# Float32 weight forms and the sums' places in a tile of their own

## The chip, the core and the metric

The kernel runs on one core of one Trainium2 chip. The metric is the device time of one execution in microseconds. A core has a matrix engine (PE, TensorE), three engines for elementwise work (DVE is VectorE, ACT is ScalarE, POOL is GpSimd), and a queue for transfers (SP, SyncE); ACT issues transfers as well. Each engine works through its own list of instructions in order and waits on semaphores where a value of another engine is needed. PE reads its operands from on-chip memory (128 partitions) and writes sums to PSUM. In the profile PEld is the loading of a weight into PE, an instruction of its own.

## What is computed

Causal attention over a window of 128 positions with a slope for each head, then a feed-forward layer in which two projections are multiplied:

```
scores = scale * q @ k.T                       # 8 batches, 8 heads, 576 positions, 64 wide
scores = where(0 <= rel < 128, scores - slopes * abs(rel), -1e9)
attn   = exp(scores - max);  attn = attn / (sum(attn) + 1e-9)
x      = attn @ v                              # -> 4608 tokens x 512
out    = ((x @ w_a) * (x @ w_b)) @ w_out       # 512 -> 1536 -> 512
```

The weights arrive as 64-bit floating point numbers and the result is float32.

## The kernel before, in words

**Batches.** The eight batches are worked one after the other, and the attention of batch b + 1 runs beside the feed-forward layer of batch b. The attention of batch 0 stands alone at the start (its lines are around 520 to 680), and beside it the weights are prepared. The feed-forward layer of batch 0 is `first_up` (twelve strips f of 128 hidden columns, 48 matmuls each: two halves of the tokens, two weights, and 12 partial products) and `first_down`. Later batches use `up_plain` or `up_fast` for each strip and `down` behind it. A product of two fp16 numbers split in a high and a low part takes three matmuls (high x high, high x low, low x high); `terms` issues the six of one block of weights against one block of x, for both k halves.

**The tile of weights.** `wup` holds, for each of the 12 strips, seven blocks of weights; a block is 128 columns for two k halves, each as a high and a low fp16 part (L83). Blocks 0 to 3 are the weights themselves: `w_a` in 0 and 1, `w_b` in 3 and 2. Blocks 4 to 6 are sums and differences of these, which only `up_fast` reads. That function makes a strip from seven products in place of eight, and is used for the first six strips of batch 2, ten strips of batch 3 and all strips from batch 4 on. A strip of blocks 4 to 6 is therefore free in the first two batches, and the kernel uses it for other things.

**From 64 bits to fp16.** A load n brings 1024 raw 64-bit numbers a partition into `raws[n % 3]`, which lies in the tile of the down weights, `wdn`. Loads 0 to 11 are strips of up weights, 12 to 17 pairs of strips of down weights. `convert(n)` makes float32 bit patterns from them in three DVE instructions (L130, L132, L133), written to `forms[n % 6]`. `forms[n]` is blocks 4 and 5 of strips 2n **and** 2n + 1 of `wup`: two runs of 512 float32 numbers a partition, with the blocks 6 of the first strip and 0 to 3 of the second between them.

```
wup = const.tile([P, NF, 7, 2, 2, P], F16, name="wup")
forms = [wup[:, 2 * n:2 * n + 2, 4:6, :, :, :].rearrange("p m a c k f -> p m (a c k f)").bitcast(F32) for n in range(NF // 2)]
```

For up weights ACT squares the forms (L139), PE sums the squares (L155), DVE and POOL make a power of two from the largest (L160 and `power_scale`), and `split_up` writes the fp16 parts into blocks 0 to 3 (ACT L147 the high part, DVE L148 the low one). For down weights one scale serves all: `down_weights` adds up all squares, sends the sum through a matmul with ones into the tile `wtot` (L100 and L101), works out `ratio` (L225), and then splits strip by strip into `wdn` (L229 on ACT, L230 on DVE), which overwrites the raws.

**Sums.** `sums_of_weights` makes blocks 4 to 6 in batches 1 to 3. For each strip and each k half POOL adds the high and low part of blocks 0 to 3 in float32 (L246) and forms block 3 again and the three new ones (L247 to L250); ACT writes the four high parts into blocks 3 to 6 with one copy of 4 x 128 numbers a partition (L255), and DVE the four low parts with one subtraction (L256). POOL's float32 results need a place for a while: for strips below 8 that is one of four `spare` places, in blocks 4 and 5 of strips 8 to 11, in turn, later a work tile `ws32`.

**Order.** SP's list is in the order of the source for the first batch, and PE's list for all later batches. All other lists are put in order by a scheduler that simulates the time of each instruction and takes the waits between instructions into account. Such a wait is made where two accesses overlap in a tile.

**Attention, as far as it appears below.** For a pair of heads: load q and k; for batches from 2 on, square and sum (L322), scale and split into `qkh` and `qkl` (L339, L340), and lay the parts out anew with transfers (L348 to L351); scores on PE (L376 for batch 1, L380 later); bias and maximum on DVE (L384); exponential on ACT (L385); normalize (`rin`: L394, L398) and split into the fp16 parts of `phl` (L401 on ACT, L402 on DVE); one transfer that transposes `phl` into `pT`; the product with v on PE (L503); and out of PSUM on ACT (L416). In the feed-forward layer L788 and L790 take the up products out of PSUM into `rc` (the hidden values), and L844 and L845 split these into h.

Of the kernel before, what the change touches and what calls it, by code (L numbers as in the profile page):

```python
# [11 lines left out]
F32 = mybir.dt.float32  # L12
F16 = mybir.dt.float16
# [5 lines left out]
ALU = mybir.AluOpType  # L19
# [3 lines left out]
DM, DF = 512, 1536  # L23
P = 128
NPAIR = H // 2
NKC = DM // P
NF = DF // P
NE = DM // P
HT = S // 2
# [17 lines left out]
def attention_then_bilinear_ffn(ctx: ExitStack, tc: tile.TileContext, qT, kT, vP, w_a, w_b, w_out, rel, slopes2, outT):  # L47
    nc = tc.nc
    vec, act, pe, pool, sp = nc.vector, nc.scalar, nc.tensor, nc.gpsimd, nc.sync

    const = ctx.enter_context(tc.tile_pool(name="const", bufs=1))
# [28 lines left out]

    wup = const.tile([P, NF, 7, 2, 2, P], F16, name="wup")  # L83
    wdn = const.tile([P, NF, 2, DM], F16, name="wdn")

    raws = [wdn[:, 4 * n:4 * n + 4, :, :].rearrange("p a c f -> p (a c f)").bitcast(I64).rearrange("p (m n) -> p m n", m=2) for n in range(3)]
    forms = [wup[:, 2 * n:2 * n + 2, 4:6, :, :, :].rearrange("p m a c k f -> p m (a c k f)").bitcast(F32) for n in range(NF // 2)]
    xs = const.tile([P, 8, 2, 2, HT], F16, name="xs")
    sup = const.tile([P, NF, 2], F32, name="sup")
    ratio = const.tile([P, NF], F32, name="ratio")  # L90
# [112 lines left out]
    def down_weights():  # L203

        sums = small.tile([P, NF // 2], F32, tag="wos", name="wos", bufs=1)
        for n in range(NF // 2 + 1):
            conv = convert(NF + n) if n < NF // 2 else iter(())
            next(conv, None)
            yield
            next(conv, None)  # L210
            if n:
                squares(NF + n - 1, accum_out=sums[:, n - 1:n])
                if n + 2 < NF // 2:
                    load_weights(NF + n + 2, (w_out[2 * n + 4], w_out[2 * n + 5]), sp)
            yield
        sab = small.tile([P, NF], F32, tag="sab", name="sab", bufs=1)
        vec.tensor_tensor(out=sab, in0=sup[:, :, 0], in1=sup[:, :, 1], op=ALU.mult)
        vec.tensor_reduce(out=smin, in_=sab, op=ALU.min, axis=AX)
        vec.reciprocal(sab, sab)
        s1 = small.tile([P, 1], F32, tag="wo1", name="wo1", bufs=1)  # L220
        vec.tensor_reduce(out=s1, in_=sums, op=ALU.add, axis=AX)
        tot = ps_at.tile([P, 512], F32, tag="at", name="wtot")
        total(tot[:, 0:1], s1)
        power_scale(so, tot[:, 0:1], 1.01, 15)
        vec.tensor_scalar(out=ratio, in0=sab, scalar1=smin, scalar2=so, op0=ALU.mult, op1=ALU.mult)  # L225
        yield
        for f in range(NF):
            s, x = ratio[:, f:f + 1], forms[f // 2][:, f % 2, :]
            act.activation(wdn[:, f, 0, :], x, AF.Copy, scale=s)  # L229
            vec.scalar_tensor_tensor(out=wdn[:, f, 1, :], in0=x, scalar=s, in1=wdn[:, f, 0, :], op0=ALU.mult, op1=ALU.subtract)  # L230
            yield

    def sums_of_weights():


        spare = cycle([wup[:, f, 4:6, :, :, :].rearrange("p a c k f -> p (a c k f)").bitcast(F32).rearrange("p (s f) -> p s f", s=4) for f in range(8, NF)])

        def place():
            return next(spare) if f < 8 else work.tile([P, 4, P], F32, tag="t", name="ws32", bufs=4)

        late = []
        for f, k in [(f, k) for f in range(NF) for k in range(2)] + [(None, None)] * 1:
            if f is not None:
                a, z = place(), place()
                with tc.issue_after(last_bias[0].ins):
                    pool.tensor_tensor(out=a, in0=wup[:, f, 0:4, 0, k, :], in1=wup[:, f, 0:4, 1, k, :], op=ALU.add)  # L246
                pool.tensor_tensor(out=z[:, 0, :], in0=a[:, 3, :], in1=a[:, 2, :], op=ALU.add)  # L247
                pool.tensor_tensor(out=z[:, 2, :], in0=a[:, 0, :], in1=a[:, 3, :], op=ALU.subtract)
                pool.tensor_tensor(out=z[:, 1, :], in0=z[:, 0, :], in1=a[:, 0, :], op=ALU.subtract)
                pool.tensor_tensor(out=z[:, 3, :], in0=a[:, 1, :], in1=z[:, 1, :], op=ALU.subtract)  # L250
            late.append((f, k, z))
            if len(late) > 1:
                g, m, x = late.pop(0)
                with tc.issue_after(last_main[0].ins):
                    act.copy(wup[:, g, 3:7, 0, m, :], x)  # L255
                vec.tensor_tensor(out=wup[:, g, 3:7, 1, m, :], in0=x, in1=wup[:, g, 3:7, 0, m, :], op=ALU.subtract)  # L256
            yield


# [587 lines left out]
    def terms(ps, a, b, first, last):  # L847

        ks = [(k, wi, xi) for k in range(2) for wi, xi in ((0, 0), (0, 1), (1, 0))]
        for n, (k, wi, xi) in enumerate(ks):  # L850
            pe.matmul(ps[:, 0:HT], wup[:, a[0], a[1], wi, k, :], xs[:, b, xi, k, :], start=(first and n == 0), stop=(last and n == len(ks) - 1), skip_group_check=True)  # L851

    def up_plain(st, f, h):

# [221 lines left out]
```

## Time and profile before

| | |
|---|---|
| median of 3 runs | 999.38 us (998.4 to 1001.05) |
| the profiled execution, its own time | 1000.43 us |
| its span in the trace | 998.6 us |
| mean clock granted to PE | 0.987 |
| instructions | 23811 |
| moved by transfers | 102.82 MB, 103 GB/s on average |

The engines' busy time by stage, in us, from the windows of the trace:

| stage (us of the span) | length | PE | DVE | ACT | POOL | clock |
|---|---|---|---|---|---|---|
| 0 to 120, attention of batch 0, most weights | 120 | 108.08 | 98.04 | 88.09 | 21.05 | 0.94 |
| 120 to 165, first up projection | 45 | 34.80 | 42.88 | 33.91 | 8.07 | 0.89 |
| 165 to 210, first down projection | 45 | 44.33 | 25.48 | 25.95 | 6.96 | 1.00 |
| 210 to 460, batches 1 to 3 in the main, with the sums | 250 | 244.81 | 181.35 | 175.23 | 103.01 | 1.00 |
| 460 to 998.6, the rest | 538.6 | 532.91 | 319.98 | 310.54 | 116.42 | 1.00 |

The span is the time from the first to the last recorded instruction; the execution's own time is a little longer. A row of the timeline or of a group names the engine, the tiles written and read (written<-read), the line in the kernel and the number of instructions. An instruction that had to wait carries in brackets how long and for which instruction. L12 is line 12 of the kernel.

### The profile page before, as it was taken

How to read it: one execution, taken by the hardware profiler on the slowest of the kernel's cores; microseconds unless marked ns; L12 is line 12 of the kernel's file. 1: busy time of each engine (PE TensorE's matmuls, PEld its weight loads, DVE VectorE, ACT ScalarE, POOL GpSimd, SP SyncE). 2: the span in 40 equal slices, each digit the busy share in tenths (PEclk: the TensorE clock that was granted, in tenths of full speed). 3: DMA queues.
4: the chain of work that ended last, by engine and by line, in shares of the span. 5: the costliest groups of instructions: out<-in, count | busy, mean ns of one | idle time of the engine just before them, and what ended most of it. 6: DMA issues, size and time to landing. Idle time of an engine off the chain costs nothing.

```text
span 998.6 us, 23811 instructions
## 1 busy us (share of the span) xinstructions
PE 964.9 (97%) x9339; PEld 749.9 (75%) x9339; DVE 667.7 (67%) x1843; ACT 633.7 (63%) x1705; POOL 255.5 (26%) x309
## 2 busy tenths in 40 slices
PE   7899959999999999999999999999999999999998
PEld 5567747777877777777777777777777777877776
DVE  5979999468878567786778677666677476524530
ACT  5967769567666757766776867677666766413321
POOL 1211212022655312452226123121223022211100
PEclk8999979999999999999999999999999999999999
DMA  8424753474346343473533643374335532210001
GB/s 316 170 110 189 230 154 61 110 187 84 65 97 139 95 90 70 86 178 75 99 75 96 160 91 65 76 192 107 68 72 97 161 67 44 49 37 8 1 13 36
DMA packets 148432, 102.82 MB, mean 103 GB/s; under 512 B 120032, under 2 KB 128352, under 8 KB 147296
## 3 DMA queue, kind: packets, MB, share of 16 engines
q1 hardware_dynamic: 138816, 91.77, 37.8%
q10 hardware_dynamic: 9504, 9.54, 3.0%
q8 instruction: 73, 1.20, 0.5%
q14 instruction: 39, 0.32, 0.1%
HBM read 48.33 MB, written 9.44 MB: 58 GB/s over the span
## 4 chain that ended last, share of the span: by engine, by line
PE 69%; DVE 14%; DMA 7%; ACT 6%; issue 3%; SPq 0%; POOL 0%; ACTq 0%; DVEq 0%
PE ch L851 19%; PE dn_ps L947 16%; PE p L851 14%; PE up_ps L851 11%; PE x_ps L503 4%; PE sc_ps L380 3%; DMA v<-in_vP 3%; DVE phl L402 2%; DMA pT<-phl 2%; PE dn_ps L814 2%; DVE wup L133 1%; DVE wup L148 1%; DVE wup L132 1%; DVE t L384 1%; ACT vsq L278 1%
## 5 line engine op out<-in xcount | busy, mean ns | idle before, releaser
L851 PEld LDWEIGHTS <-wup 128*128 128x128 f16 x4224 | 408.9, 98 | 125.3 <-DVE wup L133 10.5
L947 PE MATMUL dn_ps<-h,wdn 128*128 128x288 f16 x2016 | 254.4, 286 | 0.0
L947 PEld LDWEIGHTS <-wdn 128*128 128x128 f16 x2016 | 194.0, 98 | 51.8
L851 PE MATMUL ch<-xs,wup 128*128 128x288 f16 x1536 | 221.8, 286 | 1.8 <-ACT rc L876 1.3
L851 PE MATMUL up_ps<-xs,wup 128*128 128x288 f16 x1536 | 196.6, 288 | 11.0 <-DVE wup L133 10.2
L851 PE MATMUL p<-xs,wup 128*128 128x288 f16 x1152 | 172.6, 286 | 0.0
L906 POOL TENSOR_TENSOR rc<-rc,row 128x288 f32<-128x288 f32 x64 | 62.5, 976 | 279.7 <-DVE row L904 263.7
L385 ACT ACTIVATE t<-t,mn 128x192 f32<-128x192 f32 (+2 forms) x252 | 107.1, 427 | 25.2 <-DVE mn L384 25.0
L402 DVE SCALAR_TENSOR_TENSOR phl<-t,rin,phl 128x192 f16<-128x192 f32 (+2 forms) x252 | 107.5, 467 | 19.7 <-ACT phl L401 19.5
L844 ACT CAST h<-rc 128x576 f16<-128x576 f32 x96 | 64.2, 669 | 70.3 <-DVE rc L911 36.7
L401 ACT ACTIVATE phl<-t,rin 128x192 f16<-128x192 f32 (+2 forms) x252 | 88.8, 425 | 31.1 <-DMA pT<-phl 17.7
L845 DVE TENSOR_TENSOR h<-rc,h 128x576 f16<-128x576 f32 x90 | 69.0, 767 | 31.1 <-ACT h L844 30.1
L384 DVE CUSTOM_DVE_ANT_0 t<-sc_ps,bias,neg 128x192 f32<-128x192 f32 (+2 forms) x216 | 73.8, 390 | 8.0 <-PE sc_ps L380 7.9
L438 DVE TENSOR_TENSOR xs<-v,xs 128x576 f16<-128x576 f32 x52 | 49.0, 955 | 22.3 <-ACT xs L437 22.1
L952 ACT ACTIVATE row<-dn_ps,oi 128x288 f32<-128x288 f32 x56 | 27.6, 494 | 55.9 <-PE dn_ps L947 55.8
L888 ACT ACTIVATE row<-ch,g 128x288 f32<-128x288 f32 x64 | 31.8, 497 | 48.8 <-PE ch L851 48.8
L883 DVE TENSOR_TENSOR rc<-p,rc 128x288 f32<-128x288 f32 x64 | 29.1, 455 | 44.1 <-PE p L851 34.6
L361 POOL TENSOR_SCALAR bias<-rel_sb,ninv,sl_sb 128x192 f32<-128x192 f32 x24 | 20.3, 844 | 121.6 <-DVE mn L384 121.6
L432 POOL TENSOR_TENSOR xq<-xq,sq 128x576 bf16<-128x576 bf16 x22 | 29.5, 1341 | 83.7 <-ACT sq L431 83.7
L911 DVE SCALAR_TENSOR_TENSOR rc<-rc,g,ch 128x288 f32<-128x288 f32 x64 | 32.7, 511 | 23.6 <-PE ch L851 23.4
L385 ACT ACTIVATION_READ_ACCUMULATOR t<-t,mn 128x1 f32 x252 | 47.6, 189 | 0.0
L437 ACT CAST xs<-v 128x576 f16<-128x576 f32 x52 | 34.1, 668 | 16.6 <-POOL v L456 9.4
(148 smaller groups left out, 1260.3 us busy)
## 6 DMA issues: line engine op xcount, KB each, us to landing
v<-in_vP SPq DMA_DIRECT2D x8, 1280.0 KB, 6.5
out<-row ACTq DMA_DIRECT2D x62, 144.0 KB, 1.8
qk<-in_qT SPq DMA_DIRECT2D x28, 288.0 KB, 4.1
qk<-in_kT SPq DMA_DIRECT2D x28, 288.0 KB, 4.6
wdn<-in_w_a SPq DMA_DIRECT2D x12, 512.0 KB, 5.1
wdn<-in_w_b SPq DMA_DIRECT2D x12, 512.0 KB, 5.9
wdn<-in_w_out SPq DMA_DIRECT2D x12, 512.0 KB, 4.4
qst<-qkh SPq DMA_DIRECT2D x24, 144.0 KB, 2.8
```

The costliest lines, as they stand in the source:

```text
L384: vec.tensor_tensor_reduce(out=t[:, c:c + w], in0=ps[:, c:c + w], in1=o.bias[:, WIN - w:WIN], scale=-0.125 if o.b == 1 else o.neg, scalar= ...
L385: act.activation(t[:, c:c + w], t[:, c:c + w], AF.Exp, bias=o.mn[:, n:n + 1], scale=-1.0, accum_out=o.sm[:, n:n + 1])
L401: act.activation(phl[:, 0, pc:pc + w], e, AF.Copy, scale=s)
L402: vec.scalar_tensor_tensor(out=phl[:, 1, pc:pc + w], in0=e, scalar=s, in1=phl[:, 0, pc:pc + w], op0=ALU.mult, op1=ALU.subtract)
L437: act.copy(xs[:, n, 0, :, :], src)
L438: vec.tensor_tensor(out=xs[:, n, 1, :, :], in0=src, in1=xs[:, n, 0, :, :], op=ALU.subtract)
L503: last = pe.matmul(xp[oc // 512][64 * h:64 * h + 64, o0:o0 + w], vt[0:rows, c:c + 64], probs(pt, rows, blocks, h), start=(n == 0 and first ...
L844: act.copy(h[:, f, :, 0, :], hid)
L845: eng.tensor_tensor(out=h[:, f, :, 1, :], in0=hid, in1=h[:, f, :, 0, :], op=ALU.subtract)
L851: pe.matmul(ps[:, 0:HT], wup[:, a[0], a[1], wi, k, :], xs[:, b, xi, k, :], start=(first and n == 0), stop=(last and n == len(ks) - 1), ski ...
L906: pool.tensor_tensor(out=x0, in0=x0, in1=mid, op=ALU.mult)
L947: pe.matmul(ps[:, 0:HT], wdn[:, f, wi, e * P:(e + 1) * P], h[:, f, t, hi, :], start=(m == 0 and n == 0), stop=(m == NF - 1 and n == 2))
```

## The change

`wup` keeps four blocks a strip. Blocks 4 to 6 become blocks 0 to 2 of a new tile `wsum` with the same twelve strips. Seen as float32, `wsum` is one run of 9216 numbers a partition, here named `flat`. The forms are now nine pieces of 1024 in a row, which fill it exactly, in place of six pairs of strips. Load n goes to `forms[n % 9]`, and `down_weights` reads load 12 + k at `forms[(12 + k) % 9]`. The spare places are the last third of `flat`, strips 8 to 11 with all their blocks, as six pieces of 512 in place of four.

Since block 3 and blocks 4 to 6 of a strip now lie in two tiles, the copy and the subtraction at the end of `sums_of_weights` are each made twice: 128 numbers a partition for block 3, 384 for the others. There are 24 of each pair, so 24 more instructions on ACT and 24 more on DVE. `terms` chooses the tile by the block's number. Nothing that is computed changes.

```diff
--- before.py
+++ after.py
@@ -80,11 +80,13 @@
 
 
 
-    wup = const.tile([P, NF, 7, 2, 2, P], F16, name="wup")
+    wup = const.tile([P, NF, 4, 2, 2, P], F16, name="wup")
+    wsum = const.tile([P, NF, 3, 2, 2, P], F16, name="wsum")
     wdn = const.tile([P, NF, 2, DM], F16, name="wdn")
 
     raws = [wdn[:, 4 * n:4 * n + 4, :, :].rearrange("p a c f -> p (a c f)").bitcast(I64).rearrange("p (m n) -> p m n", m=2) for n in range(3)]
-    forms = [wup[:, 2 * n:2 * n + 2, 4:6, :, :, :].rearrange("p m a c k f -> p m (a c k f)").bitcast(F32) for n in range(NF // 2)]
+    flat = wsum.rearrange("p f a c k q -> p (f a c k q)").bitcast(F32)
+    forms = [flat[:, 2 * DM * n:2 * DM * n + 2 * DM].rearrange("p (m f) -> p m f", m=2) for n in range(9)]
     xs = const.tile([P, 8, 2, 2, HT], F16, name="xs")
     sup = const.tile([P, NF, 2], F32, name="sup")
     ratio = const.tile([P, NF], F32, name="ratio")
@@ -225,7 +227,7 @@
         vec.tensor_scalar(out=ratio, in0=sab, scalar1=smin, scalar2=so, op0=ALU.mult, op1=ALU.mult)
         yield
         for f in range(NF):
-            s, x = ratio[:, f:f + 1], forms[f // 2][:, f % 2, :]
+            s, x = ratio[:, f:f + 1], forms[(NF + f // 2) % len(forms)][:, f % 2, :]
             act.activation(wdn[:, f, 0, :], x, AF.Copy, scale=s)
             vec.scalar_tensor_tensor(out=wdn[:, f, 1, :], in0=x, scalar=s, in1=wdn[:, f, 0, :], op0=ALU.mult, op1=ALU.subtract)
             yield
@@ -233,7 +235,7 @@
     def sums_of_weights():
 
 
-        spare = cycle([wup[:, f, 4:6, :, :, :].rearrange("p a c k f -> p (a c k f)").bitcast(F32).rearrange("p (s f) -> p s f", s=4) for f in range(8, NF)])
+        spare = cycle([flat[:, n:n + 4 * P].rearrange("p (s f) -> p s f", s=4) for n in range(8 * 6 * P, 12 * 6 * P, 4 * P)])
 
         def place():
             return next(spare) if f < 8 else work.tile([P, 4, P], F32, tag="t", name="ws32", bufs=4)
@@ -252,8 +254,10 @@
             if len(late) > 1:
                 g, m, x = late.pop(0)
                 with tc.issue_after(last_main[0].ins):
-                    act.copy(wup[:, g, 3:7, 0, m, :], x)
-                vec.tensor_tensor(out=wup[:, g, 3:7, 1, m, :], in0=x, in1=wup[:, g, 3:7, 0, m, :], op=ALU.subtract)
+                    for w, z in ((wup[:, g, 3:4], x[:, 0:1, :]), (wsum[:, g], x[:, 1:4, :])):
+                        act.copy(w[:, :, 0, m, :], z)
+                for w, z in ((wup[:, g, 3:4], x[:, 0:1, :]), (wsum[:, g], x[:, 1:4, :])):
+                    vec.tensor_tensor(out=w[:, :, 1, m, :], in0=z, in1=w[:, :, 0, m, :], op=ALU.subtract)
             yield
 
 
@@ -847,8 +851,9 @@
     def terms(ps, a, b, first, last):
 
         ks = [(k, wi, xi) for k in range(2) for wi, xi in ((0, 0), (0, 1), (1, 0))]
+        w = wup[:, a[0], a[1]] if a[1] < 4 else wsum[:, a[0], a[1] - 4]
         for n, (k, wi, xi) in enumerate(ks):
-            pe.matmul(ps[:, 0:HT], wup[:, a[0], a[1], wi, k, :], xs[:, b, xi, k, :], start=(first and n == 0), stop=(last and n == len(ks) - 1), skip_group_check=True)
+            pe.matmul(ps[:, 0:HT], w[:, wi, k, :], xs[:, b, xi, k, :], start=(first and n == 0), stop=(last and n == len(ks) - 1), skip_group_check=True)
 
     def up_plain(st, f, h):
 
```

Lines behind the changed ones move: up to the old L230 by 2 (L133 is L135, L221 is L223), from the old L261 on by 4 (L376 is L380, L402 is L406), and from `terms` on by 5 (L851 is L856).

The first place is on PE, at the end of an attention product of batch 1 (`x_ps`) in the first up projection, where strip 9 of that projection begins. Before:

```order
L503 LDWEIGHTS vhl
L503 MATMUL x_ps<-pT,vhl 64x64
L376 MATMUL sc_ps<-qkl,qkh 64x192 [waits DVE_49,PE_49]
L376 MATMUL sc_ps<-qkl,qkh 64x192 x3
L851 LDWEIGHTS wup [waits DVE_49]
L851 MATMUL up_ps<-xs,wup 128x288
L851 LDWEIGHTS wup
```

And after the change:

```order
L507 LDWEIGHTS vhl
L507 MATMUL x_ps<-pT,vhl 64x64
L856 LDWEIGHTS wup
L856 MATMUL up_ps<-xs,wup 128x288 [waits DVE_49]
L856 LDWEIGHTS wup
L856 MATMUL up_ps<-xs,wup 128x288
```

The load of the weights of strip 9 waited for DVE and no longer does; the first matmul waits for DVE now, as the first of several groups does. The four score matmuls (`sc_ps`) moved behind 24 up matmuls.

The second place is the total of the squares of the down weights, on DVE and on PE. DVE before, from the conversion of the last but one load (`wos` are the sums of squares, `wo` their sum, `c` its copy for PE; numbers behind a name tell buffers apart):

```order
L133 SCALAR_TENSOR_TENSOR wup<-wdn,wup 128x2x512
L130 TENSOR_SCALAR wup<-wdn 128x2x512
L398 RECIPROCAL rin<-rin 128x7
L132 SCALAR_TENSOR_TENSOR wup<-wdn,wup 128x2x512
L133 SCALAR_TENSOR_TENSOR wup<-wdn,wup 128x2x512
L402 SCALAR_TENSOR_TENSOR phl<-t,rin,phl 128x64
L402 SCALAR_TENSOR_TENSOR phl<-t,rin,phl 128x128
L402 SCALAR_TENSOR_TENSOR phl<-t,rin,phl 128x192 x5
L221 TENSOR_REDUCE wo_1793<-wos 128x1
L790 SCALAR_TENSOR_TENSOR rc<-rc,g,up_ps 128x288
L100 CAST c_1796<-wo_1793 128x1
```

DVE after the change:

```order
L132 TENSOR_SCALAR wsum<-wdn 128x1024
L135 SCALAR_TENSOR_TENSOR wsum<-wdn,wsum 128x1024
L794 SCALAR_TENSOR_TENSOR rc<-rc,g,up_ps 128x288
L134 SCALAR_TENSOR_TENSOR wsum<-wdn,wsum 128x1024
L398 TENSOR_SCALAR rin<-sm 128x7
L794 SCALAR_TENSOR_TENSOR rc<-rc,g,up_ps 128x288
L135 SCALAR_TENSOR_TENSOR wsum<-wdn,wsum 128x1024
L402 RECIPROCAL rin<-rin 128x7
L794 SCALAR_TENSOR_TENSOR rc<-rc,g,up_ps 128x288
L223 TENSOR_REDUCE wo_1794<-wos 128x1
L406 SCALAR_TENSOR_TENSOR phl<-t,rin,phl 128x64
L102 CAST c_1797<-wo_1794 128x1
```

A conversion now covers one run of 1024 in place of 2 x 512. Three products of the hidden values (L790, now L794) stand ahead of the sum, and the splits of the probabilities (L402, now L406) stand behind the copy but for the first.

On PE, the matmul that makes `wtot` stands about 100 rows (weight loads included) behind the place above before, and about 250 rows behind it after the change, where these rows surround it:

```order
L856 MATMUL up_ps<-xs,wup 128x288
L103 LDWEIGHTS ones_73 [waits DVE_49]
L103 MATMUL wtot<-c_1797,ones_73 128x1 [waits PE_49]
L380 MATMUL sc_ps<-qkl,qkh 64x192 [waits PE_49]
L380 MATMUL sc_ps<-qkl,qkh 64x192 x3
L507 LDWEIGHTS vhl [waits DMAHW1_49]
```

Before, 49 of the up matmuls of strips 9 to 11 stood ahead of it, now 124 of these 144 do.

The third place is on ACT, around the last pair of heads of batch 1. Before:

```order
L385 ACTIVATE t,sm<-t,mn 128x192 x2
L416 ACTIVATE v<-x_ps 128x512
L416 ACTIVATE v<-x_ps 128x64
L431 ACTIVATE sq<-v 128x576
L385 ACTIVATE t,sm<-t,mn 128x192 x2
L322 ACTIVATE qkl,qs<-qk 128x1152
L401 ACTIVATE phl<-t,rin 128x192 x4
L385 ACTIVATE t,sm<-t,mn 128x64
```

After the change:

```order
L420 ACTIVATE v<-x_ps 128x512
L420 ACTIVATE v<-x_ps 128x64
L435 ACTIVATE sq<-v 128x576
L389 ACTIVATE t,sm<-t,mn 128x192 x2
L405 ACTIVATE phl<-t,rin 128x192 x4
L326 ACTIVATE qkl,qs<-qk 128x1152
L389 ACTIVATE t,sm<-t,mn 128x64
```

The squares of the next batch's q and k (L322, now L326), which wait for a load, moved from ahead of four splits of probabilities (L401, now L405) to behind them. SP's list is the same in both programs.

## The prediction

> **What bounds the kernel now.** I read the page first: busy shares, the slices, the chain.
>
> ```profile
> PE 964.9 (97%) x9339; PEld 749.9 (75%) x9339; DVE 667.7 (67%) x1843; ACT 633.7 (63%) x1705; POOL 255.5 (26%) x309
> PE   7899959999999999999999999999999999999998
> PEclk8999979999999999999999999999999999999999
> PE 69%; DVE 14%; DMA 7%; ACT 6%; issue 3%; SPq 0%; POOL 0%; ACTq 0%; DVEq 0%
> ```
>
> PE is busy in nearly every slice. Only slice 5, 125 to 150 us, has a hole, and there the granted clock dips as well. A change that takes nothing from PE's own work can win little outside that hole. So I asked for stages, and for who made PE wait in the first 160 us.
>
> ```profile
> 120.00:131.00 11.00, 11.00 (x122) 8.03 (x118) 11.00 (x27) 8.01 (x24) 3.20 (x2) 1.00 0.54 193
> 131.00:141.00 10.00, 0.08 (x2) 0.00 (x0) 10.00 (x17) 4.81 (x11) 1.70 (x1) 0.64 0.70 174
> 150.00:160.00 10.00, 10.00 (x113) 7.91 (x112) 9.69 (x23) 10.00 (x22) 1.71 (x2) 1.00 0.01 2
> 160.00:170.00 10.00, 10.00 (x97) 6.73 (x98) 9.67 (x33) 8.73 (x25) 4.88 (x3) 1.00 0.70 107
> 240.00:260.00 20.00, 20.00 (x201) 15.61 (x200) 17.24 (x41) 15.39 (x40) 12.27 (x17) 1.00 0.64 129
> PE up_ps L851 <- DVE wup L133: 10.2, 1, 10.2
> PE tr_ps L590 <- ACT t L584: 6.7, 5, 1.7
> ```
>
> The columns of a stage are its length, then busy time of PE, PEld, DVE, ACT and POOL, the clock, and DMA. From 131 to 141 us PE does nothing while DVE works without a break. It is one wait of 10.2 us, an up-projection matmul waiting for a conversion of weights (L133). The next largest, 6.7 us in five pieces, is in the first attention and the change does not touch it. The timelines show both sides.
>
> ```profile
> 130.21 0.87 PE L376 MATMUL sc_ps<-qkl,qkh 64*64 64x192 f32 x8
> 141.28 7.55 PE L851 MATMUL up_ps<-xs,wup 128*128 128x288 f16 x49 [10.20 <-DVE wup L133]
> 149.57 5.93 PE L851 MATMUL up_ps<-xs,wup 128*128 128x288 f16 x47
> 156.90 3.11 PE L851 MATMUL up_ps<-xs,wup 128*128 128x288 f16 x24
> 160.75 3.11 PE L851 MATMUL up_ps<-xs,wup 128*128 128x288 f16 x24
> 164.64 1.63 PE L814 MATMUL dn_ps<-h,wdn 128*128 128x288 f16 x12
> 122.24 3.10 DVE L148 SCALAR_TENSOR_TENSOR wup<-wup,sup 128x512 f16<-128x512 f32 x3
> 140.02 1.21 DVE L133 SCALAR_TENSOR_TENSOR wup<-wdn,wup 128x1024 uint32<-128x1024 uint32 x1
> ```
>
> After the wait 49 + 47 + 24 + 24 = 144 up matmuls remain, twelve groups of 12, so three strips: PE stood before strip f = 9. Its fp16 weights had long been split: the three L148s that end at 125.34 us (122.24 + 3.10) are the last of all. What it waits for is an L133 that ends at 141.23 us (140.02 + 1.21). By its place in DVE's order that is the third operation of load n = 16, a down weight, written to forms[4]. forms[4] is blocks 4 and 5 of strips 8 **and** 9. Its values are no input of strip 9's blocks 0 to 3, but from its first to its last address it runs across them. I take the wait as one for an overlap that exists only if the region is taken as a span. The order of the two programs agrees: before, that weight load is the only one of wup with a wait of its own; after, none has one.
>
> **The change part by part.**
>
> *The stall, removed:* 10.2 us. The matmuls behind it also ran slowly.
>
> ```profile
> 141.00:144.50 3.50, 3.22 (x15) 2.09 (x16) 3.47 (x7) 2.82 (x9) 0.00 (x0) 0.55 0.89 206
> 144.50:148.70 4.20, 4.20 (x37) 3.33 (x34) 2.62 (x10) 2.64 (x7) 0.00 (x0) 1.00 0.25 55
> ```
>
> The clock was 0.55 for 3.5 us after the idle time, then 1.00. The 49 matmuls lasted until 148.67, 7.4 us; at the 3.04 us per 24 of the later row (156.90 to 159.94) they take 6.2. That is 1.2 us more, so 11.4 us in all. The Trainium skill, "TensorE: Matmul & The Clock Gate", Part 1: The HAM clock gate, says that after an idle window of some 3.4 us the array runs at half rate until it was busy for about as long; the trace agrees in kind (0.55 for about 3.5 us). By that rule the second term would be 1.7 us, an estimate from the page, and the forecast 0.5 us lower.
>
> *What is late next: the down weights.* PE would reach the first down matmul at 164.6 - 11.4 = 153.2 us. The new order puts the small matmul wtot, which the scale of the down weights needs, behind some 124 of the 144 matmuls: 130.2 + 124 x 0.127 + 0.8 for four scores = 146.7 us.
>
> ```profile
> 145.59 1.06 ACT L139 ACTIVATE wdn<-wup 128x1024 bf16<-128x1024 f32 x1
> 147.29 0.15 DVE L100 CAST c<-wo 128x1 bf16<-128x1 f32 x1
> 151.98 4.38 ACT L229 ACTIVATE wdn<-wup,ratio 128x512 f16<-128x512 f32 x7
> 152.72 4.73 DVE L230 SCALAR_TENSOR_TENSOR wdn<-wup,ratio,wdn 128x512 f16<-128x512 f32 x7 [0.24 <-ACT wdn L229]
> ```
>
> Its input was ready at 147.4 us. In the new order six phl pieces that stood ahead of it come later and three L790 come earlier: 6 x 0.31 - 3 x 0.43, about 0.6 us less. So wtot waits for nothing, or under 1 us. The first weights are ready some 6 us after it, as before (153.4 against 147.4), and then one strip each 0.63 us on ACT and 0.68 on DVE, while PE needs 1.5 us per strip (164.64 to 166.2). I take 0, with 1 us at the end of the range.
>
> *Contiguous conversions:* the same 54 instructions, in one run of 1024 in place of two of 512.
>
> ```profile
> L132 DVE SCALAR_TENSOR_TENSOR wup<-wdn,wup 128x1024 int32<-128x1024 int32 x18 | 23.1, 1282 | 0.1
> L130 DVE TENSOR_SCALAR wup<-wdn 128x1024 int32<-128x1024 int32 x18 | 13.4, 744 | 4.3 <-DMA wdn<-in_w_b 4.3
> ```
>
> No row shows the new form. At best all run as L130 does, which brings nothing, since PE no longer waits for them; at worst L130 slows to L132's 1282 ns, 0.54 us for each of the ten that follow 78 us, and wtot comes up to 5.4 us later. Nearest is the same instruction: I take 0. The six more places (nine forms for six, six spare places for four) free DVE of waits that the trace does not show: 0.
>
> *Later, with PE ahead:* from 150 to 170 us ACT and DVE have no room, so they can't follow by the whole 11.4 us. What PE needs next is the first scores of batch 2.
>
> ```profile
> 168.76 1.26 ACT L339 ACTIVATE qkh<-qk,own 128x1152 f16<-128x1152 f32 x1 [1.27 <-DVE own L337]
> 173.86 0.46 SPq L351 DMA_DIRECT2D qkl<-qkl  x1
> qkl<-qkl SPq DMA_DIRECT2D x1, 144.0 KB, 2.3
> 183.06 0.22 PE L380 MATMUL sc_ps<-qkh,qst 128*64 128x64 f16 x2
> 179.88 1.16 ACT L322 ACTIVATE qkl<-qk 128x1152 bf16<-128x1152 f32 x1 [4.24 <-DMA qk<-in_kT]
> 183.04 9.03 DMA pT<-phl
> ```
>
> They are in place at 173.86 + 0.46 + 2.3 = 176.6 us, read at 183.06. With PE 11 us ahead they are wanted at about 172. Following ACT's new order row by row, L339 comes some 2 us earlier (the L229s now start at 150 us, and two L844, two L788 stand elsewhere): ready at 174.5, PE waits 1.5 us in two places. If ACT gains nothing, it waits 4.3; if all, 0. I take 1.5. Next comes the last product of batch 1 with its transposed probabilities, whose transfer took 9.03 us from 183.04. Before, the four phl pieces stood behind L322, which waited 4.24 us for a load; now they stand ahead of it, so the transfer starts some 8 us earlier, lands at 182 to 184, and PE wants it at 182.4: 0 to 1.5 us, I take 0.8. Behind it PE's order is the old one, and everything starts from PE again.
>
> *Two copies for one:* 24 copies on ACT and 24 subtractions on DVE are each cut in a piece of 128 and one of 384.
>
> ```profile
> L255 ACT CAST wup<-wup 128x512 f16<-128x512 f32 x16 | 9.9, 616 | 0.0
> L437 ACT CAST xs<-v 128x576 f16<-128x576 f32 x52 | 34.1, 668 | 16.6 <-POOL v L456 9.4
> L114 DVE TENSOR_SCALAR sv<-r 128x1 int32<-128x1 int32 x8 | 1.2, 151 | 0.2
> L256 DVE TENSOR_TENSOR wup<-wup 128x512 f16<-128x512 f32 x16 | 14.5, 909 | 6.3 <-ACT wup L255 6.3
> ```
>
> Between 512 and 576 elements ACT needs 52 ns more, so a copy has about 0.2 us that do not shrink with it; on DVE an instruction of one element bounds that at 0.15. At most 24 x 0.35 = 8.4 us, if all fell on PE's path; 0 if PE covers them, as in 240 to 260 us, where DVE is busy 17.24 of 20 and PE all 20. I take five of them at 0.15: 0.7 us. The Trainium skill speaks against this edit ("Perfetto Trace Analysis", Optimizing Scalar/DVE Operations): about 60 ns on DVE and 93 ns on ScalarE are spent per instruction, and larger operations help where the engine is saturated. By its figures the estimate is 24 x 0.153 = 3.7 us if all counted, and 994.0 us in place of the forecast.
>
> **Sum:** 11.4 - 1.5 - 0.8 - 0.7 = 8.4 us. The profiled execution took 1000.43 us (span 998.6 and 1.83 around it), 1 us above the median of 999.38; it becomes 992.0, the median 991.0.
>
> **Rivals.** *Half is given back.* ACT at 10.00 of 10 and DVE at 9.69 after 150 us speak for it: scores 4.3, transfer 1.5, copies five at 0.35 = 1.7; 11.4 - 7.5 = 3.9, so 995.5. Against it: PE's order moved L322 and the weights' scale in PE's favour.
>
> *Another wait takes the place.* If wtot or the weights slip by 8 us or more (conversions 5.4 later, and six L402 late), PE stands before the down projection instead: 997.5 to 1000. Against it: PE's row at 164.64 had no wait, and the weights were 11 us early.
>
> *The wait isn't from the span*, but from a true input: then nothing goes but places, 999.4. Against: L148 ended at 125.3.
>
> *Slower.* The second subtraction of each of the 24 pairs holds DVE's queue for its own copy on ACT. The scores' maxima (L384) and the hidden products (L864) stand behind it, and PE waits for those. Today DVE waits for such a copy
>
> ```profile
> DVE wup L256 <- ACT wup L255: 9.4, 9, 2.1
> ```
>
> 1.04 us at a time. At half of that per pair it costs 24 x 0.52 = 12.5 us against 9.1 won: 1002.8. It turns at 0.38 us a pair. Against: DVE has 2.8 us free of 20 there.
>
> **How the numbers follow.** The forecast has 0.64 (987 to 994), half given back 0.17, another wait 0.09, no effect 0.04, slower 0.06. The range 987.0 to 996.5 begins with nearly all of the 11.4 us and 1 us for orders not priced, ends where the half case ends, and leaves out 0.2. Within 0.3% (3 us, about what a measurement can tell from no change): 0.09 + 0.04 = 0.13. Faster: 0.64 + 0.17 = 0.81. Slower: 0.06.
>
> **What would show it.** Right: no idle PE between 131 and 141 us, clock 1.00 there, the first dn_ps at 152 to 154 us, the first batch-2 scores at 173 to 176, and PE 7 to 10 us ahead at each later stage. Wrong: a PE wait for wtot, wdn or L133; L130 above 0.8 us; PE idle in 220 to 460 us more than 2 us above before, with DVE waiting on L255.

## The result, and the profile after

| | before | after |
|---|---|---|
| median | 999.62 us (6 runs, 996.32 to 1002.22) | 990.35 us (6 runs, 989.74 to 993.44) |
| ratio, with its 95% interval | | 0.9912 (0.9889 to 0.9934) |
| the profiled execution | 1000.43 us | 989.81 us |
| its span | 998.6 us | 988.0 us |

The change makes the kernel about 9 us faster; the interval holds 6.6 to 11.1 us. The forecast was 991.0. All ratios compare means of executions and leave out two that lie far off: one of e5 at 2517 us, and one of the kernel before at 1017 us, timed beside e5 to e8.

The page of the changed kernel, busy time, PE's slices and granted clock, and the chain that ended last:

```profile
PE 962.1 (97%) x9339; PEld 748.9 (76%) x9339; DVE 669.0 (68%) x1867; ACT 635.6 (64%) x1729; POOL 255.3 (26%) x309
PE   7899999999999999999999999999999999999998
PEclk8999999999999999999999999999999999999999
PE 69%; DVE 12%; ACT 7%; DMA 7%; issue 3%; POOL 1%; SPq 0%; ACTq 0%; DVEq 0%
```

PE does the same work in 10.6 us less span, and slice 5 has lost its hole and its dip in the clock. The stages, in the columns of before (length, then busy PE, PEld, DVE, ACT, POOL, clock, DMA):

```profile
131.00:141.00 10.00, 10.00 (x86) 7.79 (x83) 10.00 (x18) 6.00 (x15) 2.63 (x1) 1.00 0.97 233
141.00:150.00 9.00, 5.41 (x75) 4.13 (x72) 7.79 (x22) 6.82 (x18) 2.55 (x2) 1.00 0.18 43
150.00:160.00 10.00, 9.80 (x88) 7.29 (x90) 9.93 (x31) 10.00 (x25) 0.42 (x1) 1.00 0.01 2
160.00:170.00 10.00, 10.00 (x117) 7.89 (x115) 8.41 (x26) 8.98 (x24) 2.58 (x2) 1.00 0.68 132
```

From 131 to 141 us PE is busy throughout, where it was busy for 0.08 us. In its place stands a smaller hole from 141 to 150 us. The waits of PE between 120 and 240 us name it (us in total, times, longest):

```profile
PE wtot L103 <- DVE c L102: 2.4, 1, 2.4
PE x_ps L507 <- DMA pT<-phl: 2.4, 1, 2.4
PE sc_ps L380 <- issue: 1.4, 1, 1.4
```

PE's timeline gives the places:

```profile
131.46 12.42 PE L856 MATMUL up_ps<-xs,wup 128*128 128x288 f16 x100
...
146.32 0.18 PE L103 MATMUL wtot<-c,ones 128*128 128x1 bf16 x1 [2.44 <-DVE c L102]
...
150.20 0.88 PE L380 MATMUL sc_ps<-qkl,qkh 64*64 64x64 f32 x12 [1.36 <-issue]
...
153.47 0.90 PE L818 MATMUL dn_ps<-h,wdn 128*128 128x288 f16 x6
...
172.96 0.30 PE L384 MATMUL sc_ps<-qkh,qst 128*64 128x64 f16 x4
...
183.93 1.54 PE L507 MATMUL x_ps<-pT,vhl 128*64 128x128 f16 x42 [2.44 <-DMA pT<-phl]
```

The wait for a conversion (L133, now L135) is gone altogether. To see where the time was won, I read from the timelines of PE when the first matmul of a stage starts:

| first matmul of | before | after | ahead by |
|---|---|---|---|
| up projection, batch 0 | 57.84 | 55.91 | 1.93 |
| down projection, batch 0 | 164.64 | 153.47 | 11.17 |
| up projection, batch 1 | 209.00 | 200.33 | 8.67 |
| down projection, batch 1 | 290.75 | 281.85 | 8.90 |
| up projection, batch 2 | 333.47 | 324.06 | 9.41 |
| up projection, batch 4 | 565.29 | 554.80 | 10.49 |
| down projection, batch 7 | 959.90 | 949.27 | 10.63 |

9.2 us come between 57 and 164 us, 2.5 go back in the first down projection, and 2.0 come back later. I do not count the first 1.9 us as the change's. The two programs have the same order of operations up to about 70 us. And e11 below is a program whose lists are those of the changed kernel up to about 170 us, and its execution reached the same two first places at 57.95 and 155.94 us, 2.0 and 2.5 us later than the changed kernel's. So a difference of 2 us between two profiles at the start shows little. That a small part of it belongs to the layout can't be excluded: four profiles with the old layout and the same order start the up projection at 57.8 to 59.1 us, eight with the new one at 55.8 to 58.0. Without these 1.9 us the two profiles differ by 10.63 - 1.93 = 8.7 us.

### The profile page after: what moved, and what is told of

Its sections match the earlier page's. It is cut to its first block, busy times and chain, and to the rows that moved or that the text cites. A ratio compares the mean times of both kernels' runs of the same rounds, so it can differ in the third digit from the quotient of the medians.

```text
span 988.0 us, 23867 instructions
## 1 busy us (share of the span) xinstructions
PE 962.1 (97%) x9339; PEld 748.9 (76%) x9339; DVE 669.0 (68%) x1867; ACT 635.6 (64%) x1729; POOL 255.3 (26%) x309
## 4 chain that ended last, share of the span: by engine, by line
PE 69%; DVE 12%; ACT 7%; DMA 7%; issue 3%; POOL 1%; SPq 0%; ACTq 0%; DVEq 0%
PE ch L856 19%; PE dn_ps L952 18%; PE p L856 14%; PE up_ps L856 9%; PE x_ps L507 4%; DMA v<-in_vP 4%; PE sc_ps L384 3%; DVE phl L406 2%; PE dn_ps L818 2%; ACT t L389 1%; DVE wsum L135 1%; DVE xs L442 1%; ACT phl L405 1%; DVE wsum L134 1%; DMA qk<-in_kT 1%
## 5 line engine op out<-in xcount | busy, mean ns | idle before, releaser
L856 PEld LDWEIGHTS <-wup 128*128 128x128 f16 x3072 | 296.3, 98 | 82.0 <-issue 5.7
L856 PE MATMUL up_ps<-xs,wup 128*128 128x288 f16 x1536 | 194.6, 286 | 1.1 <-ACT rc L867 0.8
L856 PEld LDWEIGHTS <-wsum 128*128 128x128 f16 x1152 | 111.7, 98 | 32.0 <-issue 2.5
L856 PE MATMUL ch<-xs,wup 128*128 128x288 f16 x768 | 115.0, 286 | 0.5 <-ACT row L893 0.5
L856 PE MATMUL p<-xs,wup 128*128 128x288 f16 x768 | 115.1, 286 | 0.0
L406 DVE SCALAR_TENSOR_TENSOR phl<-t,rin,phl 128x192 f16<-128x192 f32 (+2 forms) x252 | 104.6, 454 | 15.3 <-ACT phl L405 15.1
L856 PE MATMUL ch<-xs,wsum 128*128 128x288 f16 x768 | 111.5, 286 | 1.1 <-ACT rc L881 1.1
L405 ACT ACTIVATE phl<-t,rin 128x192 f16<-128x192 f32 (+2 forms) x252 | 88.9, 425 | 25.3 <-DMA pT<-phl 12.7
L856 PE MATMUL p<-xs,wsum 128*128 128x288 f16 x384 | 57.5, 286 | 0.0
```

Of the source, the lines that this page charges most:

```text
L405: act.activation(phl[:, 0, pc:pc + w], e, AF.Copy, scale=s)
L406: vec.scalar_tensor_tensor(out=phl[:, 1, pc:pc + w], in0=e, scalar=s, in1=phl[:, 0, pc:pc + w], op0=ALU.mult, op1=ALU.subtract)
L856: pe.matmul(ps[:, 0:HT], w[:, wi, k, :], xs[:, b, xi, k, :], start=(first and n == 0), stop=(last and n == len(ks) - 1), skip_group_check= ...
```

## The experiments

My theory was that the wait came from the span of one access that runs from strip to strip, and that the rest of the change (a tile of their own, contiguous pieces, more places, cut copies) was worth nothing. The rivals: the tile or the contiguous form did it; the wait was for a true input; the cut copies cost or gave something. A second question came up on the way: what bounds the changed kernel. All results first; the last three columns are PE's places as in the table above, first matmul of the down projection of batch 0, then up and down of batch 1, from one profile each.

| run | median us | ratio to before (95%) | down 0 | up 1 | down 1 |
|---|---|---|---|---|---|
| changed kernel | 990.35 | 0.9912 (0.9889 to 0.9934) | 153.47 | 200.33 | 281.85 |
| e1 | 997.94 | 0.9995 (0.9982 to 1.0007) | 166.07 | 209.30 | 290.81 |
| e2 | 992.51 | 0.9937 (0.9918 to 0.9957) | 155.82 | 203.89 | 285.51 |
| e3 | 999.84 | 1.0002 (0.9987 to 1.0017) | 165.47 | 210.34 | 292.16 |
| e4 | 991.25 | 0.9923 (0.9901 to 0.9945) | 154.67 | 201.59 | 282.73 |
| e5 | 997.17 | 0.9985 (0.9968 to 1.0003) | 156.85 | 205.71 | 287.94 |
| e6 | 996.66 | 0.9989 (0.9977 to 1.0001) | 148.42 | 200.92 | 287.90 |
| e7 | 997.50 | 1.0006 (0.9993 to 1.0019) | 154.67 | 199.11 | 287.78 |
| e8 | 996.54 | 0.9984 (0.9972 to 0.9995) | 153.15 | 207.00 | 287.50 |
| e9 | 992.25 | 0.9930 (0.9911 to 0.9948) | 154.30 | 203.77 | 285.81 |
| e10, the changed kernel again | 991.03 | 0.9918 (0.9897 to 0.9939) | 153.03 | 199.85 | 281.45 |
| e11 | 993.82 | 0.9944 (0.9923 to 0.9964) | 155.94 | 201.62 | 287.12 |

**e1, the kernel before with other pairs of strips.**

```diff
-forms = [wup[:, 2 * n:2 * n + 2, 4:6, ...] for n in range(NF // 2)]
+forms = [wup[:, 2 * ((n + 4) % 6):2 * ((n + 4) % 6) + 2, 4:6, ...] for n in range(NF // 2)]
```

> The kernel before, with one edit: load n takes the pair of strips (n + 4) mod 6 in place of n mod 6, so the forms still run from block 4 of one strip to block 5 of the next and lie in the same tile; no copy is split. If the 10.2 us before strip 9 are an overlap with the form of load 16 taken as a span, that form now lies on strips 4 and 5, which PE has passed: no PE wait on a conversion there, first down matmul some 9 to 11 us earlier than before (164.6), median 988 to 993. What is left to a wait of the same kind comes at strip 1, which asks for load 2, converted long before. If it is the tile of their own or the contiguous pieces that help, PE still waits some 10 us and the median stays at 998 to 1001.

The wait before strip 9 went, as the span would have it, and the time stayed. I had looked for the overlap at strip 1 only. The timeline shows it at strip 3 (at 93.19 us), where load 9 now has its form:

```profile
89.32 0.60 PE L155 MATMUL wn_ps<-wdn,ones 128*128 128x256 bf16 x4 [2.43 <-ACT wdn L139]
89.85 1.50 PE L376 MATMUL sc_ps<-qkl,qkh 64*64 64x64 f32 x12
91.28 0.27 PE L285 MATMUL vtot<-vc,ones 128*128 128x1 bf16 x4
93.19 4.85 PE L851 MATMUL up_ps<-xs,wup 128*128 128x288 f16 x24 [1.64 <-DVE wup L133]
```

PE waited 1.64 us for a conversion again and 2.43 us just ahead of it, and from 93.19 us 24 matmuls took 4.85 us in place of 3.1: the clock was 0.83 between 80 and 100 us. Further on PE waited another 4.0 us for copies of the hidden values (`rc`) and for `wtot`. So my expectation of 988 to 993 was wrong, and the run does not separate the theories as it was meant to: with six forms for eighteen loads, an overlap that is moved off one strip falls on another.

**e5, the kernel before with the conversions in halves.** This one takes the span away and moves nothing in memory. `m` runs over the two strips of a pair, for each of the three operations:

```diff
-        vec.tensor_scalar(out=t, in0=high, scalar1=3, ...)
+        for m in range(2):
+            vec.tensor_scalar(out=t[:, m], in0=high[:, m], scalar1=3, ...)
```

> The kernel before, with each of the three conversions of a load made as two instructions of 512 numbers, one for each strip of the pair. Nothing is moved in memory, no copy is split, the forms and places stay where they are; only an access no longer runs from one strip to the next. If the wait before strip 9 came from the span of one access, it is gone: PE waits under 1 us there, and against that stand some 30 more DVE instructions behind 60 us at about 0.1 us (3 us on a DVE that is full from 120 to 141 us), so wtot comes later than in the changed kernel: median 989 to 995. If the wait was for a value that strip 9 needs, or for anything of the place itself, it stays at 9 to 10 us or more: 998 to 1003.

The window of e5 from 131 to 141 us:

```profile
131.00:141.00 10.00, 10.00 (x91) 7.50 (x89) 10.00 (x25) 6.38 (x16) 3.87 (x2) 1.00 0.61 192
```

And its waits of PE from 125 to 300 us:

```profile
PE x_ps L506 <- DMA pT<-phl: 3.2, 2, 2.1
PE wtot L101 <- DVE c L100: 1.7, 1, 1.7
PE qtot L336 <- DVE both L328: 1.0, 1, 1.0
```

The wait before strip 9 is gone although forms, places and tiles are where they were. PE begins strip 9 with the first of these rows (144 up matmuls remain), and the last half of load 16 is converted in the second, 12 us later:

```profile
132.57 3.11 PE L854 MATMUL up_ps<-xs,wup 128*128 128x288 f16 x24
144.68 0.68 DVE L136 SCALAR_TENSOR_TENSOR wup<-wdn,wup 128x512 uint32<-128x512 uint32 x1
```

That settles it: strip 9 needed nothing from load 16, and a wait was made because one access ran across it. PE reached the down projection 7.8 us earlier than before, 1.6 of them from the start. But the time hardly fell. From there to the up projection of batch 1 it took 48.86 us in place of 44.36, in waits for the attention, and the median, between my two ranges, is within its interval of no change. The halves themselves cost what I had put down (two of 686, two of 681 and two of 419 ns, 3.57 us a load; 3.2 before in the same stretch).

**e9, the kernel before with halves for loads 16 and 17 only.** The edit is shown against e5.

```diff
+        parts = (0, 1) if n >= 16 else (slice(0, 2),)
-        for m in range(2):
+        for m in parts:
```

> The kernel before, with the three conversions in halves for loads 16 and 17 only: six DVE instructions more, nothing moved, no copy split. If the span of these two forms across strips 9 and 11 was the whole wait, PE waits under 1 us there and the first down matmul comes at 153 to 156 (164.6 before, 153.5 in the changed kernel). What is left of it at the end depends on the order behind it: if the chain of the attention (scores, probabilities, their transfer) has its own time between 150 and 210 us and only some orders fit it, a part is given back there, as in e5 (7.8 us ahead at the first down matmul, 3.3 at the first up matmul of batch 1), 991 to 997; if the give-back of e5 came from its 54 DVE instructions, this one keeps the gain: 989 to 991.

Six more DVE instructions in place of a new layout give 992.25 us, a ratio of 0.9930 beside the changed kernel's 0.9918 in the same comparison; the intervals overlap. PE reaches the down projection at 154.30 us. So the span of these two forms was the whole of what the change won at its place. Behind it PE waits again for the attention (`pT` 3.0 us, `sc_ps` 1.4, `qtot` 0.8), as much as in e5: from the down projection to the up projection of batch 1 it took 49.47 us, in the changed kernel 46.86. What e5 loses beside e9 lies ahead of that. From the first up to the first down matmul e5 took 100.57 us, e9 96.17, the changed kernel 97.56 and before 106.80; e5 has 48 more instructions on DVE than e9.

**e2, the changed kernel with the forms as pairs of strips in the new tile, and e4, the changed kernel with both regions in one tile.**

```diff
-forms = [flat[:, 2 * DM * n:2 * DM * n + 2 * DM]... for n in range(9)]
+forms = [wsum[:, 2 * n:2 * n + 2, 0:2, ...] for n in range(NF // 2)]
```

```diff
-wup = const.tile([P, NF, 4, 2, 2, P], F16, name="wup")
-wsum = const.tile([P, NF, 3, 2, 2, P], F16, name="wsum")
+both = const.tile([P, NF * 7 * 4 * P], F16, name="wup")
+wup = both[:, 0:NF * 16 * P]...
+wsum = both[:, NF * 16 * P:NF * 28 * P]...
```

> The changed kernel, with the forms again as six pairs of strips with a gap (two runs of 512, in blocks 4 and 5 of the new tile) and four spare places. Only the distance from blocks 0 to 3 is left of the first half of the change. If the span across blocks 0 to 3 was the cause, nothing is lost: 989 to 992, no PE wait on a conversion, conversions of 0.75, 1.2 and 1.2 to 1.3 us as before. If one run of 1024 or the three more forms help, part of the gain goes: 993 or more, and the first down matmul later than 155.

> The changed kernel, with both regions in one tile again: four blocks a strip first, the contiguous forms and sums behind them. Nothing overlaps by address. If the wait came from addresses: 989 to 992, no PE wait on a conversion. If waits are made by the tile, or two tiles lie better in memory: a wait of up to 10 us before strip 9, 994 to 1001.

Neither has a wait for a conversion. e4 agrees with the changed kernel: a tile of their own is not needed, only addresses that do not interleave. e2's median is 2 us higher. Its conversions are as long as the contiguous ones, here first the changed kernel's groups (line, tiles and shape, then busy time and mean ns), then e2's:

```profile
L135 DVE SCALAR_TENSOR_TENSOR wsum<-wdn,wsum 128x1024 uint32<-128x1024 uint32 x18 | 23.9, 1327 | 0.0
L134 DVE SCALAR_TENSOR_TENSOR wsum<-wdn,wsum 128x1024 int32<-128x1024 int32 x18 | 22.0, 1221 | 0.1
```

```profile
L135 DVE SCALAR_TENSOR_TENSOR wsum<-wdn,wsum 128x1024 uint32<-128x1024 uint32 x18 | 23.9, 1328 | 0.0
L134 DVE SCALAR_TENSOR_TENSOR wsum<-wdn,wsum 128x1024 int32<-128x1024 int32 x18 | 22.0, 1220 | 0.1
```

One run of 1024 or two of 512 makes no difference. In e2's profile the lag is 1.75 us at the first up projection, 2.35 at the first down, 3.56 at the next up, and 3.6 to 4.2 from there on. The last two steps are stretches at half clock behind the waits for `wtot` and `pT`, which the changed kernel has as well (2.4 us each), without the stretches. e2's waits, and its windows behind them:

```profile
PE wtot L103 <- DVE c L102: 2.6, 1, 2.6
PE x_ps L507 <- DMA pT<-phl: 2.0, 1, 2.0
```

```profile
150.00:154.00 4.00, 3.36 (x44) 2.73 (x41) 3.12 (x21) 4.00 (x11) 1.70 (x2) 0.62 0.01 2
187.00:192.00 5.00, 5.00 (x45) 3.31 (x40) 3.89 (x9) 5.00 (x13) 0.16 (x1) 0.66 0.09 30
```

In the changed kernel the clock is 1.00 at both places. Whether e2's six medians are higher for this reason each time I can't tell from one profile; that the pieces or the number of places account for a part of up to 2 us stays open.

**e3, the kernel before with only the copies cut.**

```diff
-act.copy(wup[:, g, 3:7, 0, m, :], x)
+for w, z in ((wup[:, g, 3:4], x[:, 0:1, :]), (wup[:, g, 4:7], x[:, 1:4, :])):
+    act.copy(w[:, :, 0, m, :], z)
```

> The kernel before, with only the copy and the subtraction of each of the 24 steps of the sums cut in two (128 and 384). The 10.2 us wait stays. If the split costs what the prediction took (five of 24 at 0.15 us): 0.7 us more than before, 1000 to 1001 beside 999.6; if all of it were on PE's path: 24 x 0.35 = 8.4 us, 1008; with the second subtraction holding DVE's queue: 24 x 0.52 = 12.5, 1012. If it frees something, as the sums' stage of the changed kernel may hint (PE came 1.7 us ahead between 209 and 565 us): 997 to 999.

A ratio of 1.0002, within 0.17% either way. The wait for load 16 is 9.9 us. In the profile the stretch between the up projections of batches 1 and 4, which holds the sums, took 355.02 us (210.34 to 565.36), before 356.29. The copies do cost busy time: in the changed kernel's groups a pair of copies takes 296 + 512 ns on ACT where one took 616, and a pair of subtractions 476 + 691 ns on DVE where one took 909. PE shows no wait for it. That the stretch became 1.3 us shorter I don't put down to the copies: e1 and e9, without them, show 355.38 and 355.37.

**e6, e7, e8 and e11: what bounds the changed kernel.** Each is the changed kernel with one number changed, aimed at one of its two remaining waits.

```diff
-weave(att.along(first_up(st, h), 49, 3.2), (weights, 0, 40, 50))
+weave(att.along(first_up(st, h), 49, 3.2), (weights, 0, 36, 50))      # e6
-weave(att.along(first_down(0, out_scale(st), h), 24, 5.15), ...)
+weave(att.along(first_down(0, out_scale(st), h), 24, 5.0), ...)       # e7
+weave(att.along(first_down(0, out_scale(st), h), 24, 5.05), ...)      # e11
-vec.tensor_reduce(out=s1, in_=sums, op=ALU.add, axis=AX)
+vec.tensor_reduce(out=s1, in_=sums[:, 0:5], op=ALU.add, axis=AX)      # e8
```

> The changed kernel, with the steps of the weights spread over the first 36 of the first up projection's steps in place of 40. This is on what bounds it now: PE waits 2.4 us for the total of the down weights and 1.4 us for scores behind it, and 2.4 us for the transposed probabilities. If the conversions stand too late in DVE's order, the wait for the total goes and the time falls by 2 to 5 us (986 to 988.5). If DVE as a whole is the bound up to the total, PE waits as long for PSUM banks or scores instead, 989 to 993.

> The changed kernel, with the pace of the attention beside the first down projection at 5.0 in place of 5.15: the last product of batch 1 stands behind 204 down matmuls in place of 180, 3 us later for PE. If its 2.4 us wait is for a transfer that has its own time, it goes, and the time falls by 2 to 2.5 us (988), up to 4 where a half-speed stretch followed the wait. If what stands behind it is then late in turn (scores of batch 2, first up matmul of batch 1), nothing is won: 990 to 992.

> The changed kernel, with the sum of squares of the last of six loads of down weights left out of their total, so the scale does not wait for the last ACT square. The total comes 1 to 3 us earlier. If the total is what PE needs, its 2.4 us wait goes or is under 1 us and the first down matmul comes 2 to 4 us earlier (150 to 152), 986.5 to 988.5. If the splits of the down weights or DVE set that place, the first down matmul stays at 153 to 155 and the time at 989 to 992.

> The changed kernel, with the pace beside the first down projection at 5.05: the last product of batch 1 stands behind 192 down matmuls in place of 180, 1.5 us later, and SP's order stays the same (in e7 it changed as well, and scores waited 2.4 us for a transfer that had moved behind others). If e7's loss was that transfer, the wait for the probabilities shrinks to about 0.9 us and the time falls by 1 to 1.5 us: 988 to 990. If batch 2's scores stand too late once they are moved at all, 991 to 996, with DVE's maxima waited for near 270 us as in e7 (3.0 us).

By their medians all four lost 3 to 7 us, and e6, e7 and e8 lie above every range that I had written down. The waits of PE between 120 and 300 us, for e6, e7 and e8 in turn:

```profile
PE qtot L337 <- DVE both L329: 5.7, 2, 3.6
PE x_ps L507 <- DMA pT<-phl: 3.5, 2, 2.0
PE wtot L103 <- DVE c L102: 1.1, 1, 1.1
```

```profile
PE sc_ps L384 <- DVE mn L388: 3.9, 2, 3.0
PE sc_ps L384 <- DMA qkh<-qkh: 2.4, 1, 2.4
PE wtot L103 <- DVE c L102: 2.2, 1, 2.2
```

```profile
PE x_ps L507 <- DMA pT<-phl: 6.9, 2, 5.2
PE wtot L103 <- DVE c L102: 2.6, 1, 2.6
```

e6 did what it was to do: PE was at the down projection at 148.42 us, 5 us earlier, and lost all of it and 6 us more by 288 us, waiting for the squares of q and k (`both`) and for `pT`. In e7 the wait for `pT` is gone and the down projection is 2.4 us shorter (44.44 us in place of 46.86), as expected; then scores come late, and the next stage is 7.2 us longer (88.67 in place of 81.52). e11 repeats that at half the size with SP's order unchanged, so e7's moved transfer was not the whole cause. In e8 the total still waited 2.6 us, because the copy for it (L102) stands behind the last conversion in DVE's order; leaving out a load's squares moved other instructions, and `pT` came later. The end is much the same each time: PE at the down projection of batch 1 at 287 to 288 us, and 281 to 282 in the changed kernel. (e11 had started 2.0 us late, and so lost less on the way.)

e5 to e8 ran on another chip than e1 to e4, and the changed kernel was not timed there. I ran it again beside e9 and e11, on a third.

> The changed kernel again, unedited, beside the others on one chip. If e6 to e8 lost what they lost by their edits and not by the chip: 989 to 992, and 281 to 284 us at the first down matmul of batch 1. If the chip made it: 995 to 998.

The result repeats: 0.9918, and 281.45 us at the down projection of batch 1. This does not test the chip of e6 to e8, but their profiles do. From the down projection of batch 1 to that of batch 7 they took 666.6, 668.2 and 668.0 us, the changed kernel 667.4 and e10 667.6. So that chip was not slower there, and what they lost, they lost in the waits ahead of it.

## Why the prediction was right

**The stall (10.2 us) and the slow matmuls behind it (1.2 us)** went as worked out. 131 to 141 us is full and the clock is 1.00 from 120 to 160 us. That the wait came from a span was argued from the order of the programs; e5 and e9 show it.

**The down weights: put at 0, with 1 us at the end of the range; PE waited 2.44 us for `wtot` and 1.36 us for scores soon after.** The forecast had PE at `wtot` at 146.7 us and the copy for it ready 0.6 us before 147.4, at 146.8. Less the 1.9 us of the start these are 144.8 and 144.9. PE was there at 143.88 (146.32 - 2.44), 0.9 us earlier, and the copy ended at 146.26, 1.4 us later. That chain on DVE is the mis-sized step. The three products of the hidden values that come ahead of the copy were counted rightly. These are the windows of that one line's instructions up to the copy, before (L790) and after (L794), with DVE's busy time as the second number:

```profile
131.00:147.20 16.20, 0.85 (x2) 0.68 0.69 166
```

```profile
131.00:146.10 15.10, 2.46 (x5) 1.00 0.76 180
```

They are 1.6 us more, where 1.3 had been taken. But the last conversion took 2.20 us in place of 1.23, which no term held; here it is before, then after, with the sum of the squares and the copy behind it:

```profile
143.12 1.23 DVE L133 SCALAR_TENSOR_TENSOR wup<-wdn,wup 128x1024 uint32<-128x1024 uint32 x1
```

```profile
142.26 2.20 DVE L135 SCALAR_TENSOR_TENSOR wsum<-wdn,wsum 128x1024 uint32<-128x1024 uint32 x1
145.67 0.16 DVE L223 TENSOR_REDUCE wo<-wos 128x1 f32<-128x6 f32 x1 [0.72 <-ACT wdn L141]
146.11 0.15 DVE L102 CAST c<-wo 128x1 bf16<-128x1 f32 x1
```

And the six splits of the probabilities (L402) that left saved 1.3 us in place of 1.9, from the end of that conversion to the end of the copy, since DVE now stood 0.72 us for ACT's square. Why the conversion took longer is open. For the 1.36 us the profile names no releaser, so it is not shown that they belong to the down weights. The rival in which another wait takes the stall's place is true in kind, at a third of its size or less. Up to the first down matmul 11.4 us had been expected, and 9.2 came (11.17 less the 1.93 of the start). Of these, 0.8 us are no gain: eight score matmuls and a `qtot` that stood ahead of that place before stand behind it now.

**Batch 2's scores and the transposed probabilities: 2.3 us given back expected, 2.5 found**, of which 0.8 are the matmuls just named and 1.7 waits, nearly all in one place. The scores start at 172.96 us without a wait (1.5 expected). The probabilities landed at 183.9 us, within the 182 to 184 forecast, and PE stood there from 181.5 (0.8 expected, 2.44 measured), because the scores had not held it.

**The cut copies: 0.7 us given back expected, none found** (e3). One such cut costs 0.19 us on ACT, as estimated, and 0.26 on DVE, where 0.15 had been called the bound; PE covers both. The stages from batch 1 on gained 2.0 us (10.63 - 8.67) that no term held. They are not shown to be the change's: from the up projection of batch 1 to the down projection of batch 7 the changed kernel took 748.9 us and before 750.9, but e1, e3 and e9, which keep the old layout, took 748.6, 749.0 and 749.2.

**The sum.** 8.4 us expected, 8.7 found from the first up projection on; by the medians 9.3, and 8.0 beside e10. The main term is right, and the errors of the others (-2.2, -0.2 and +2.7) nearly cancel, which is luck: without the 2.0 us that are not shown to be the change's, these profiles give 6.7. The rival in which half is given back deserved more than its 0.17: e5, e9 and e11 are kernels without the stall in which the attention took back between 1 us and nearly everything.

**The signs.** No idle time at 131 to 141 us, the first down matmul between 152 and 154, the first conversion at 746 ns: as written. PE was 8.7 to 10.6 us ahead later, where 7 to 10 had been written. From 220 to 460 us PE was idle for 3.0 us, before for 5.2, so the sign against the cut copies did not come. A wait for `wtot` had been named as a sign against; it came, and was too small to decide.

## What to carry to other kernels

When an engine waits for a value that it does not read, look at the first and the last address of the two accesses, not at their elements: in this program an access that jumps over a region was ordered against all of it. Keep scratch data out of the gaps of data that are read, or cut the access at the gap; here six more instructions did nearly what a new layout did. Then ask who gets the work that the freed engine now makes, since an engine at 97% hides chains that are nearly as long as its own.

## What the runs showed of the hardware

**A wait of 2 to 2.6 us can bring a stretch at half clock, or not.** In the changed kernel two waits of 2.44 us left the clock at 1.00. In e2 waits of 2.6 and 2.0 us at the same places were followed by clocks of 0.62 and 0.66 over 4 and 5 us, and in e9 a wait of 2.15 us by this product, which takes 1.54 us elsewhere:

```profile
190.82 2.53 PE L507 MATMUL x_ps<-pT,vhl 128*64 128x128 f16 x42 [2.15 <-DMA pT<-phl]
```

One program can show both. Up to the wait for `wtot` e10 and e11 are the changed kernel: 2.44 us in that kernel's profile and 2.08 in e10's left the clock at 1.00, and 2.49 us in e11's were followed by 0.67 over 4 us.

The Trainium skill ("TensorE: Matmul & The Clock Gate", Part 1: The HAM clock gate) says that the monitor's window of some 3.4 us runs freely and does not start with the program, so that it depends on the run where in a window an event falls. That fits a wait that is followed by a slow stretch in one execution and not in the next. It also says that the clock drops after an idle window; here 2.15 us of idle time were enough (clock 0.55 from 190.8 to 194.2 us in e9).

**Executions of one program differ by 2 us in the first 60 us.** Up to the first up projection e7, e10 and e11 are the changed kernel, and got there at 57.38, 55.82 and 57.95 us.
